# Both heads' last 64 keys in one slot, and early queries centred with tokens on partitions, in a linear-attention and gated-feed-forward kernel

## The chip, the cores and the metric

The kernel runs on one core of one Trainium2 chip. The metric is the device time of one execution in microseconds; three runs of the kernel before gave 1332.12, 1333.95 and 1334.01 (median 1333.95). Lower is better. PE is the matrix engine, PEld its weight loads, DVE the vector engine, ACT the scalar engine, POOL the general engine and SP the engine whose queue issues most DMA transfers.

## The reference

Attention with positive random features, then a gated feed-forward layer, all in float32:

```python
def phi(x):                                   # q, k, v: 8 batches, 8 heads, 576 tokens, 64 wide
    proj = einsum('bhsd,df->bhsf', x, w_phi)  # 128 features
    proj = proj - max(abs(proj), axis=-1, keepdims=True)
    return concatenate([exp(proj), exp(-proj)], axis=-1)
kv = einsum('bhsf,bhsd->bhfd', phi(k), v);  z = sum(phi(k), axis=2)
num = einsum('bhsf,bhfd->bhsd', phi(q), kv)
den = einsum('bhsf,bhf->bhs', phi(q), z) + 1e-06
x = (num / den) as 4608 tokens x 512
out = (silu(x @ w_gate) * (x @ w_val)) @ w_out   # 512 -> 1536 -> 512
```

The largest absolute value is taken over the 128 features of one token, so it is a reduction along the features.

## The kernel before, in words

**Pairs.** Two heads of one batch make a pair; there are 32 (`attention(i, rank)`, L329). Inputs lie with the 2 x 64 head dimensions on partitions, so one pair's keys are a tile `kin` of 128 x 576, its queries `qin` likewise. `wbd` (128 x 256) is the projection as a block diagonal: head 0's features in its first 128 columns, head 1's in the others.

**Keys.** The 576 tokens stand in five slots of 128 that begin at 0, 128, 256, 384 and 448 (`SLOTS`, L30). The last slot overlaps the one before by 64 tokens, whose rows in the value tile `vf` are zero. In three groups (two slots, two, one: `K_GROUPS`) a slot's 128 tokens are the stationary operand and `wbd` streams past (L270 `kin`), DVE takes the largest value (L383) and subtracts it (L388), ACT makes both exponentials (L395), and PE multiplies into the bank `kv` (L407): per slot, head and sign one product of 128 features by 128 columns, 64 of values and 64 of ones. The ones give `z` repeated 64 times, so that the numerators' product also makes the denominators. ACT copies the bank to `kvs` (L417).

**Queries.** `wbd`'s half for a head is stationary and 288 tokens stream, so features lie on partitions (L270 `qin`). ACT copies the four results to `qx` (L449). The largest value over partitions is found by DVE: two 32 x 32 block transposes (L455), a reduction (L459), six small copies and maxima over the partition groups (L462 to L467), a transpose that spreads the result (L471) and the subtraction (L473). ACT makes two exponentials of 128 x 1152 into `qe` and `qx` (L475, L476). Then four numerator products on PE (`kvs`), copies to `num` and `den` on ACT (L514, L516), and on DVE a transpose, a reciprocal, a transpose back and a product (L523 to L527). ACT and DVE split the result into a high and a low part `xh`, `xl` (L539, L541).

**Early and late pairs.** The first eight pairs (`EARLY_PAIRS`) multiply in plain float32. Each such product stands in the trace as two matmul records and two weight loads. The other 24 split operands into high and low parts and multiply three times in the type `fp32r`, one record each; they share only the `kv` product's plain float32 with the early ones. An early pair may use five PSUM banks for work, a late one two.

**The feed-forward layer.** Chunks of 384 tokens go through twelve slices of 128 hidden units. The first layer (`gv`) is 24 matmuls of 384 columns a slice, the second (`o`) nine of 512 columns. Three chunks come from the early pairs. Their first layer runs while the weights, which arrive as float64, are converted: 36 pieces, each with two steps on ACT (L292, L307) and seven on DVE (L293 to L308).

**The order.** `Plan` lays out every engine's instructions ahead of time by simulating them with assumed costs (`dve`, `act`, `pe`, `pe32`). Of the ready steps the one of the lowest rank goes first: a pair's number is its rank, the weights' slices have 3.0, 5.0, 6.5 and up (`W_RANKS`), feed-forward products come after all pairs that are ready. Where PE has nothing, the planner puts in a dummy product (`nothing`, L706 and L708) that keeps PE awake. Each engine then runs its own list in order, so a step that waits holds all behind it.

Of the kernel before, what the change touches and what calls it, by code (L numbers as in the profile page):

```python
# [8 lines left out]
F32 = mybir.dt.float32  # L9
# [20 lines left out]
SLOTS = [0, 128, 256, 384, 448]  # L30
K_GROUPS = [(0, 2), (2, 4), (4, 5)]

# [148 lines left out]
def favor_attention_moe(ctx: ExitStack, tc: tile.TileContext, qT, kT, v, w_phi, wg, wv, wo, out):  # L181
# [23 lines left out]
    kin, qin = [sb("kin", [P, S])] * 2, [sb("qin", [P, S])] * 2  # L205

    vf = [sb("vf", [P, 5, 2, P])] * 2
# [4 lines left out]
    kvl = sb("kvl", [P, 4 * P], F32R)  # L212
    km = sb("km", [P, 4], F32, 4)
# [21 lines left out]
    k_parts = lambda: later("ks", "qx1", [P, 2, S])  # L235
    q_parts = lambda: later("qs", "qe1", [P, 2, S])
    kv_high = lambda: later("kvh", "kvs1", [P, 4 * P])

# [9 lines left out]
    wbd, wst = sb("wbd", [P, 2 * NF]), osb[1][:, :NF]  # L248
# [4 lines left out]
    for hi, lo, w in ((wbd_hi, wbd_lo, wbd), (wst_hi, wst_lo, wst)):  # L253
        nc.scalar.copy(hi, w)
        nc.vector.tensor_tensor(out=lo, in0=w, in1=hi, op=ALU.subtract)
    for h in range(2):
        nc.gpsimd.memset(vf[0][:, :, h, (1 - h) * D:(2 - h) * D], 1.0)
    nc.gpsimd.memset(vf[0][0:D, 4], 0.0)
# [70 lines left out]
    def attention(i, rank):  # L329
# [11 lines left out]
        k_in = add("SP", P * S * 4, lambda: nc.sync.dma_start(kin[j], kT[b, pr]), [last.get(("kin", i - 1))], rank)  # L341
# [11 lines left out]
        if early:  # L353
            k_ready = [k_in]
        else:
            k_hi = add("ACT", act(S), lambda: nc.scalar.copy(k_parts()[:, 0], kin[j]),
                       [k_in, last.get(("khi", i - 1)), *(use("qx") if i == EARLY_PAIRS else ())], rank)
            k_lo = add("DVE", dve(S), lambda: vec.tensor_tensor(
                out=k_parts()[:, 1], in0=kin[j], in1=k_parts()[:, 0], op=ALU.subtract), [k_hi], rank)
            k_ready = [k_hi, k_lo]  # L360
            last["kin", i] = k_lo
        kv_steps = []
        for g, (t0, t1) in enumerate(K_GROUPS):
            w = t1 - t0
            key = ("k", i, g)
            buf = (3 * i + g) % 2
            view = lambda key=key, w=w: work[plan.bank[key]][:, :w * 256].rearrange("p (t f) -> p t f", f=NF)

            def project(t0=t0, t1=t1, key=key):
                o = work[plan.bank[key]]  # L370
                for t in range(t0, t1):
                    c = slice(SLOTS[t], SLOTS[t] + P)
                    acc = o[:, (t - t0) * 256:(t - t0 + 1) * 256]
                    if early:
                        matmuls([(acc, kin[j][:, c], wbd, True, True)])
                    else:
                        khi, klo = (k_parts()[:, n, c] for n in range(2))
                        matmuls([(acc, khi, wbd_hi, True, False), (acc, khi, wbd_lo, False, False),
                                 (acc, klo, wbd_hi, False, True)])

            kproj = add("PE", w * (pe32(256) if early else 3 * pe(256)), project, k_ready, rank, take=key)
            m = km[(3 * i + g) % len(km)]
            kmax = add("DVE", dve(256 * w), lambda w=w, m=m, view=view: vec.tensor_reduce(  # L383
                out=m[:, :2 * w], in_=view(), axis=AX.X, op=ALU.max, apply_absolute_value=True),
                       [kproj, last.get(("km", 3 * i + g - 4))], rank)

            def centre(w=w, m=m, view=view, buf=buf):
                vec.tensor_tensor(  # L388
                    out=kp[buf][:, :w, :, 1].rearrange("p t h f -> p (t h) f"), in0=view(), op=ALU.subtract,
                    in1=m[:, :2 * w].rearrange("p (n o) -> p n o", o=1).broadcast_to([P, 2 * w, NF]))  # L390

            def exponential(s, w=w, buf=buf):
                x = kp[buf][:, :w, :, 1].rearrange("p t h f -> p (t h) f")
                o = kp[buf][:, :w, :, s].rearrange("p t h f -> p (t h) f")
                nc.scalar.activation(o, x, AF.Exp, scale=-1.0 if s else 1.0)  # L395

            ksub = add("DVE", dve(256 * w), centre, [kmax, last.get(("kp", 3 * i + g - 2))], rank, give=key)
            e0 = add("ACT", act(256 * w), lambda f=exponential: f(0), [ksub], rank)
            e1 = add("ACT", act(256 * w), lambda f=exponential: f(1), [e0], rank)
            last["km", 3 * i + g] = ksub  # L400

            def values(t0=t0, t1=t1, buf=buf, g=g):
                for t in range(t0, t1):
                    for h in range(2):
                        for s in range(2):
                            o = ps_kv[:, (2 * h + s) * P:(2 * h + s + 1) * P]
                            nc.tensor.matmul(o, kp[buf][:, t - t0, h, s], vf[j][:, t, h],  # L407
                                             start=t == 0 and h + s == 0, stop=t == 4 and h + s == 2)

            kv = add("PE", 4 * w * pe32(P), values, [e1, *v_in, last.get(("kv", i - 1)), *kv_steps[-1:]], rank)  # L410
# [3 lines left out]
        if early:  # L414
            last["kin", i] = kproj
        last["vf", i] = kv_steps[-1]
        kvc = [add("ACT", act(4 * P), lambda: nc.scalar.copy(kv_high() if split else kvs[j], ps_kv),  # L417
                   [kv_steps[-1], *use("kvs")], rank)]
        if split:
            kvc.append(add("DVE", dve(4 * P), lambda: vec.tensor_tensor(out=kvl, in0=ps_kv, in1=kv_high(), op=ALU.subtract),  # L420
                           kvc, rank))
# [3 lines left out]
        copies, q_lo = [], []  # L425
        for h in range(2):
            ra, rb = rows(h)
            if early:
                lo = q_in
            else:  # L430
# [4 lines left out]
            q_lo.append(lo)  # L435
            for part in range(2):
                key = ("q", i, h, part)
                c = slice(part * SH, (part + 1) * SH)

                def project(h=h, c=c, key=key):  # L440
                    acc = work[plan.bank[key]][:, :SH]
                    if early:
                        matmuls([(acc, wbd[:, h * NF:(h + 1) * NF], qin[j][:, c], True, True)])
                    else:
# [3 lines left out]
                pj = add("PE", pe32(SH) if early else 2 * pe(SH), project, [lo], rank, take=key)  # L448
                copies.append(add("ACT", act(SH), lambda h=h, c=c, key=key: nc.scalar.copy(  # L449
                    qx[j][:, h, c], work[plan.bank[key]][:, :SH]), [pj, *use("qx")], rank, give=key))  # L450
            last["qs", h, i] = pj
        last["qin", i] = pj if early else q_lo[-1]
        flat = lambda t: t.rearrange("p h s -> p (h s)")
        blocks = lambda t: flat(t).rearrange("p (a j) -> p a j", j=32)
        turns = [add("DVE", dve(S), lambda h=h: vec.transpose(qe[j][:, h], qx[j][:, h]),  # L455
                     [*copies[2 * h:2 * h + 2], *use("qe")], rank) for h in range(2)]

        def largest():
            vec.tensor_reduce(out=qm, in_=blocks(qe[j]), axis=AX.X, op=ALU.max, apply_absolute_value=True)  # L459

        def over_groups():
            vec.tensor_copy(qu[0:64], qm[64:128])  # L462
            vec.tensor_tensor(out=qm[0:64], in0=qm[0:64], in1=qu[0:64], op=ALU.max)
            vec.tensor_copy(qu[0:32], qm[32:64])
            vec.tensor_tensor(out=qu[0:32], in0=qm[0:32], in1=qu[0:32], op=ALU.max)
            vec.tensor_copy(qu[32:64], qu[0:32])
            vec.tensor_copy(qu[64:128], qu[0:64])  # L467

        mx = add("DVE", dve(2 * S), largest, turns, rank)
        mg = add("DVE", 6 * 170, over_groups, [mx], rank)  # L470
        back = add("DVE", dve(2 * S), lambda: vec.transpose(  # L471
            blocks(qe[j]), qu.rearrange("p (a o) -> p a o", o=1).broadcast_to([P, 2 * NBL, 32])), [mg], rank)
        qc = add("DVE", dve(2 * S), lambda: vec.tensor_tensor(out=flat(qx[j]), in0=flat(qx[j]), in1=flat(qe[j]),  # L473
                                                              op=ALU.subtract), [back], rank)
        f0 = add("ACT", act(2 * S), lambda: nc.scalar.activation(flat(qe[j]), flat(qx[j]), AF.Exp), [qc], rank)  # L475
# [284 lines left out]
```

## Time and profile before

| what | value |
|---|---|
| median of three runs | 1333.95 us |
| the profiled execution's own time | 1333.89 us |
| its span, first to last instruction | 1331.8 us |
| PE busy | 1289.6 us (97%) |
| DVE busy | 900.7 us (68%) |
| ACT busy | 656.6 us (49%) |
| mean granted PE clock | 0.989 |

Busy times of PE overlap: a matmul's record runs from its start to the end of its way through the array, and the next one starts before that. What one matmul costs in a stream is the distance from its start to the next start, and that is read from the timeline, where consecutive equal instructions are one row with a count. A row's second column is the time from the first start to the last end.

### The profile page before, as it was taken

How to read it: one execution, taken by the hardware profiler on the slowest of the kernel's cores; microseconds unless marked ns; L12 is line 12 of the kernel's file. 1: busy time of each engine (PE TensorE's matmuls, PEld its weight loads, DVE VectorE, ACT ScalarE, POOL GpSimd, SP SyncE). 2: the span in 40 equal slices, each digit the busy share in tenths (PEclk: the TensorE clock that was granted, in tenths of full speed). 3: DMA queues.
4: the chain of work that ended last, by engine and by line, in shares of the span. 5: the costliest groups of instructions: out<-in, count | busy, mean ns of one | idle time of the engine just before them, and what ended most of it. 6: DMA issues, size and time to landing. Idle time of an engine off the chain costs nothing.

```text
span 1331.8 us, 19557 instructions
## 1 busy us (share of the span) xinstructions
PE 1289.6 (97%) x7517; PEld 1204.0 (90%) x7517; DVE 900.7 (68%) x1569; ACT 656.6 (49%) x1255; POOL 1.2 (0%) x7
## 2 busy tenths in 40 slices
PE   7997699999999999999999999999999999999998
PEld 6885599999888899999999999999999999999997
DVE  6999689999777788872487777752277787322222
ACT  5776543333767656661356666541276575221211
POOL 0000000000000000000000000000000000000000
PEclk9998799999999999999999999999999999999999
DMA  4324145554455433344334343344443333344433
GB/s 116 88 85 138 34 139 173 186 174 156 151 164 162 128 109 115 106 140 127 121 122 120 110 148 98 112 138 128 135 128 105 115 119 92 116 147 133 147 120 102
DMA packets 105565, 168.14 MB, mean 126 GB/s; under 512 B 46336, under 2 KB 52736, under 8 KB 105472
## 3 DMA queue, kind: packets, MB, share of 16 engines
q1 hardware_dynamic: 105152, 166.76, 40.8%
q8 instruction: 59, 0.97, 0.3%
q14 instruction: 34, 0.28, 0.1%
q10 hardware_dynamic: 320, 0.13, 0.0%
HBM read 143.26 MB, written 23.59 MB: 125 GB/s over the span
## 4 chain that ended last, share of the span: by engine, by line
PE 89%; DVE 6%; DMA 2%; ACT 1%; issue 1%; ACTq 0%; DVEq 0%
PE gv L270 44%; PE o L270 24%; PE work L270 11%; PE kv L407 10%; DMA w_lo<-wlo_dram 1%; DMA out_dram<-osb 1%; DVE kp L388 1%; DMA kin<-in_kT_dram 1%; DVE qx L473 0%; DVE qe L455 0%; DVE km L383 0%; DVE qm L459 0%; DVE qe L471 0%; PE gv L706 0%; DVE den L525 0%
## 5 line engine op out<-in xcount | busy, mean ns | idle before, releaser
L270 PE MATMUL gv<-xh,w_hi 128*128 128x384 f32 x1152 | 388.6, 337 | 3.1 <-ACT xh L539 1.8
L270 PE MATMUL gv<-xl,w_hi 128*128 128x384 f32 x1152 | 386.9, 336 | 1.2 <-DVE xl L541 1.2
L270 PE MATMUL gv<-xh,w_lo 128*128 128x384 f32 x1152 | 387.3, 336 | 0.0
L270 PEld LDWEIGHTS gv<-xh,w_hi 128*128 128x128 f32 x1152 | 216.8, 188 | 9.8 <-ACT xh L539 3.0
L270 PEld LDWEIGHTS gv<-xl,w_hi 128*128 128x128 f32 x1152 | 216.7, 188 | 6.6 <-DVE xl L541 2.0
L270 PEld LDWEIGHTS gv<-xh,w_lo 128*128 128x128 f32 x1152 | 216.5, 188 | 0.0
L606 ACT ACTIVATE th<-gv 128x384 f32<-128x384 f32 x144 | 70.8, 491 | 266.3 <-PE gv L270 263.1
L608 DVE SCALAR_TENSOR_TENSOR th<-th,gv 128x384 f32<-128x384 f32 x144 | 78.9, 548 | 154.1 <-ACT th L606 153.5
L270 PE MATMUL o<-w_lo,hh 128*128 128x512 f32 x432 | 172.1, 398 | 1.6 <-DMA w_lo<-wlo_dram 1.3
L270 PE MATMUL o<-w_hi,hh 128*128 128x512 f32 x432 | 171.4, 397 | 2.0 <-ACT osb L655 2.0
L270 PE MATMUL o<-w_hi,hl 128*128 128x512 f32 x432 | 171.3, 397 | 0.0
L407 PE MATMUL kv<-vf,kp 128*128 128x128 f32 x1280 | 159.8, 278 | 2.5 <-ACT kp L395 2.5
L407 PEld LDWEIGHTS kv<-vf,kp 128*128 128x128 f32 x1280 | 156.2, 195 | 5.5 <-ACT kp L395 3.2
L631 ACT CAST hh<-th 128x384 fp32r<-128x384 f32 x144 | 73.6, 511 | 164.4 <-DVE th L611 148.7
L611 DVE TENSOR_TENSOR th<-th,gv 128x384 f32<-128x384 f32 x144 | 79.4, 552 | 67.2 <-PE gv L270 64.7
L395 ACT ACTIVATE kp<-kp 128x512 f32<-128x512 f32 (+1 forms) x192 | 105.8, 557 | 28.8 <-DVE kp L388 26.1
L523 DVE STREAM_TRANSPOSE qe<-den 128x576 f32<-128x576 f32 x32 | 24.8, 775 | 132.5 <-ACT den L516 132.5
L632 DVE TENSOR_TENSOR hl<-th,hh 128x384 fp32r<-128x384 f32 x144 | 79.2, 550 | 32.7 <-ACT hh L631 32.1
L270 PEld LDWEIGHTS o<-w_hi,hl 128*128 128x128 f32 x432 | 81.5, 189 | 19.0
L270 PEld LDWEIGHTS o<-w_lo,hh 128*128 128x128 f32 x432 | 81.6, 189 | 16.5 <-DMA w_lo<-wlo_dram 4.1
L270 PEld LDWEIGHTS o<-w_hi,hh 128*128 128x128 f32 x432 | 81.5, 189 | 15.5 <-ACT osb L655 2.8
L514 ACT COPY num<-work 64x288 f32<-64x288 f32 x106 | 41.7, 393 | 56.1 <-PE work L270 54.8
(94 smaller groups left out, 1793.8 us busy)
## 6 DMA issues: line engine op xcount, KB each, us to landing
w_lo<-wlo_dram SPq DMA_DIRECT2D x108, 512.0 KB, 3.5
w_lo<-wlo_dram SPq DMA_DIRECT2D x132, 256.0 KB, 3.0
kin<-in_kT_dram SPq DMA_DIRECT2D x32, 288.0 KB, 3.1
qin<-in_qT_dram SPq DMA_DIRECT2D x32, 288.0 KB, 2.8
wlo_dram<-w_lo SPq DMA_DIRECT2D x36, 256.0 KB, 2.1
out_dram<-osb SPq DMA_DIRECT2D x36, 256.0 KB, 3.0
vf<-in_v_dram SPq DMA_DIRECT2D x64, 128.0 KB, 3.0
shared<-in_wg_dram SPq DMA_DIRECT2D x12, 512.0 KB, 3.5
```

The costliest lines, as they stand in the source:

```text
L270: nc.tensor.matmul(o, l, r, start=a, stop=z)
L388: vec.tensor_tensor(out=kp[buf][:, :w, :, 1].rearrange("p t h f -> p (t h) f"), in0=view(), op=ALU.subtract, in1=m[:, :2 * w].rearrange("p ...
L395: nc.scalar.activation(o, x, AF.Exp, scale=-1.0 if s else 1.0)
L407: nc.tensor.matmul(o, kp[buf][:, t - t0, h, s], vf[j][:, t, h], start=t == 0 and h + s == 0, stop=t == 4 and h + s == 2)
L514: copied.append(add("ACT", act(SH), lambda key=key, ra=ra, c=c: nc.scalar.copy(num[ra, c], work[plan.bank[key]][ra, :SH]), [nu, free], rank))
L523: t0 = add("DVE", dve(S), lambda: vec.transpose(turned, den), [*copied, *done], rank)
L606: s1 = add("ACT", act(CH), lambda: nc.scalar.activation(t_, ps_gv[0][:, :CH], AF.Tanh, scale=0.5), [ends[0], th_free[j]], FIRST)
L608: s2 = add("DVE", dve(CH), lambda: nc.vector.scalar_tensor_tensor(out=t_, in0=t_, scalar=1.0, in1=ps_gv[0][:, :CH], op0=ALU.add, op1=ALU.m ...
L611: s3 = add("DVE", dve(CH), lambda: nc.vector.tensor_tensor(out=t_, in0=t_, in1=ps_gv[1][:, :CH], op=ALU.mult), [s2, ends[1]], FIRST)
L631: s4 = add("ACT", act(CH), lambda: nc.scalar.copy(hh[b], th[j]), [made, hid_free[b]], FIRST)
L632: s5 = add("DVE", dve(CH), lambda: nc.vector.tensor_tensor(out=hl[b], in0=th[j], in1=hh[b], op=ALU.subtract), [s4], FIRST)
```

## The change

The last key slot now holds no token twice. Its 128 rows are head 0's last 64 tokens (rows 0 to 63) and head 1's (rows 64 to 127). In `kin`, now 128 x 640, columns 512 to 575 have head 0's dimensions and zero elsewhere, 576 to 639 head 1's. The stacked projection `wst` (both heads' weights in the same 128 columns) then gives 128 features a token, so the tail's projection, reduction, subtraction and exponentials are half as wide. Values carry two columns of ones in place of 64 (`D2` is 66), and the tail needs one product a sign, of 132 columns. Two ACT copies make `kvs` from the bank: the values, and the sums repeated 64 times. For late pairs the low part (`kvl`) takes two DVE steps likewise. `kin` comes in three transfers.

An early pair's queries go the keys' way: tokens stationary, `wbd` streaming 256 columns (five slots, the last overlapping), reduction and subtraction along the features into `qy`, then PE turns each 128 x 128 block with an identity matrix into PSUM, and ACT's exponentials read it there. DVE's transposes, the small maxima and the copies of the projection are gone from these pairs. Late pairs' queries are as before. The identity is made by POOL at the start, ahead of two of the five memsets of the padding; `wst` has a tile of its own.

```diff
+Q_GROUPS = [(0, 2), (2, 4), (4, 5)]
+SK = 5 * P
+D2 = D + 2
...
-    kin, qin = [sb("kin", [P, S])] * 2, [sb("qin", [P, S])] * 2
-    vf = [sb("vf", [P, 5, 2, P])] * 2
+    kin, qin = [sb("kin", [P, SK])] * 2, [sb("qin", [P, S])] * 2
+    vf = [sb("vf", [P, 5, 2, D2])] * 2
...
+    qy = sb("qy", [P, 4, NF], F32, 2)
+    ident = sb("ident", [P, P])
...
+    make_identity(nc, ident)
...
-        k_in = add("SP", P * S * 4, lambda: nc.sync.dma_start(kin[j], kT[b, pr]), ...)
+        k_in = [add("SP", P * 4 * P * 4, lambda: nc.sync.dma_start(kin[j][:, :4 * P], kT[b, pr, :, :4 * P]), ...)]
+        k_in += [add("SP", P * P, lambda r=slice(h * D, (h + 1) * D), c=4 * P + h * D: nc.sync.dma_start(
+            kin[j][r, c:c + D], kT[b, pr, r, 4 * P:]), ...) for h in range(2)]
...
             def project(t0=t0, t1=t1, key=key, tail=tail):
+                    c = slice(t * P, (t + 1) * P)
+                    acc = o[:, :NF] if tail else o[:, (t - t0) * 256:(t - t0 + 1) * 256]
                     if early:
-                        matmuls([(acc, kin[j][:, c], wbd, True, True)])
+                        matmuls([(acc, kin[j][:, c], wst if tail else wbd, True, True)])
...
             def values(t0=t0, t1=t1, room=room, tail=tail):
+                if tail:
+                    for k in range(2):
+                        nc.tensor.matmul(ps_kv[:, 2 * k * D2:2 * (k + 1) * D2], room[:, 0, k],
+                                         vf[j][:, 4].rearrange("p h d -> p (h d)"), start=False, stop=k == 1)
+                    return
                 for t in range(t0, t1):
                     for h in range(2):
-                            o = ps_kv[:, (2 * h + s) * P:(2 * h + s + 1) * P]
-                            nc.tensor.matmul(o, kp[buf][:, t - t0, h, s], vf[j][:, t, h], ...)
+                            o = ps_kv[:, (2 * k + h) * D2:(2 * k + h + 1) * D2]
+                            nc.tensor.matmul(o, room[:, 2 * (t - t0) + h, k], vf[j][:, t, h], ...)
...
-        kvc = [add("ACT", act(4 * P), lambda: nc.scalar.copy(kv_high() if split else kvs[j], ps_kv), ...)]
+        for ones in range(2):
+            kvc.append(add("ACT", act(4 * D), lambda ones=ones: nc.scalar.copy(
+                cut(kv_high() if split else kvs[j], ones), sums(ones)), ...))
...
+        if early:
+            for g, (t0, t1) in enumerate(Q_GROUPS):
+                    for t in range(t0, t1):
+                        matmuls([(o[:, (t - t0) * 256:(t - t0 + 1) * 256], qin[j][:, SLOTS[t]:SLOTS[t] + P], wbd, True, True)])
+                mx = add("DVE", dve(256 * w), ... vec.tensor_reduce(out=m[:, 4:4 + 2 * w], in_=view(), ...)
+                qc = add("DVE", dve(256 * w), centre, ...)      # qy = projection - largest
+                def turn(w=w, y=y, key2=key2):
+                    for h in range(2):
+                        for t in range(w):
+                            nc.tensor.transpose(o[:, (h * w + t) * P:(h * w + t + 1) * P], y[:, 2 * t + h], ident)
+                f0 = add("ACT", act(2 * size), lambda f=exponential: f(0), [tn, ...], rank)
+                f1 = add("ACT", act(2 * size), lambda f=exponential: f(1), [f0], rank, give=key2)
+        else:
...
```

The planner lays out all lists anew. PE's list where the third pair's projections begin (`kv` is the key-value bank, `o_` and `work_` are PSUM banks for work, `nil` is the dummy), before:

```order
L407 MATMUL kv<-vf,kp_106 128x128 x4
L270 MATMUL o_138<-wbd,kin 128x256 x2
L270 MATMUL o_140<-wbd,kin 128x256 x2
L270 MATMUL o_139<-wbd,kin 128x256
L270 MATMUL work_144<-qin,wbd 128x288
L270 MATMUL work_145<-qin,wbd 128x288
L706 MATMUL gv_142<-wbd_hi,nil 128x256 x2
L270 MATMUL work_144<-qin,wbd 128x288
L270 MATMUL work_145<-qin,wbd 128x288
L706 MATMUL gv_142<-wbd_hi,nil 128x256 x8
```

and in the changed kernel, with the turns through `ident`:

```order
L424 MATMUL kv<-vf,kp_106 128x66 x8
L424 MATMUL kv<-vf,kp_107 128x66 x8
L485 MATMUL o_141<-ident,qy_120 128x128 x4
L279 MATMUL o_142<-wbd,qin 128x256 x2
L279 MATMUL o_140<-wbd,qin 128x256
L279 MATMUL work_146<-wbd,kin 128x256 x2
L279 MATMUL work_147<-wbd,kin 128x256 x2
L417 MATMUL kv<-vf,kp_106 128x132 x2
L279 MATMUL o_141<-wst,kin 128x128
L279 MATMUL gv_143<-xh_97,w_hi_69 128x384
```

Key and query projections now stand between the `kv` products, the turns are spread among them, and the dummies at this place are gone. Over the whole stage of the early pairs the list had 72 dummies and has 20. In both kernels 42 `gv` matmuls stand ahead of the last early pair's numerators.

DVE's list for one early pair's queries, before (the first row is the second block transpose, and L308 and its like would be weight conversion):

```order
L455 STREAM_TRANSPOSE qe_112<-qx_110 128x576
L459 TENSOR_REDUCE qm<-qe_112 128x36
L462 COPY qu<-qm 64x36
L463 TENSOR_TENSOR qm<-qm,qu 64x36
L464 COPY qu<-qm 32x36
L465 TENSOR_TENSOR qu<-qm,qu 32x36
L466 COPY qu<-qu 32x36
L467 COPY qu<-qu 64x36
L471 STREAM_TRANSPOSE qe_112<-qu 128x1152
```

and now (L400 and L405 are the next pair's keys, L469 and L474 the queries):

```order
L469 TENSOR_REDUCE km_116<-o_140 128x4
L474 TENSOR_TENSOR qy_120<-o_140,km_116 128x512
L469 TENSOR_REDUCE km_117<-o_142 128x2
L474 TENSOR_TENSOR qy_121<-o_142,km_117 128x256
L400 TENSOR_REDUCE km_118<-o_141 128x4
L405 TENSOR_TENSOR kp_106<-o_141,km_118 128x4x128
L400 TENSOR_REDUCE km_119<-work_146 128x4
L405 TENSOR_TENSOR kp_107<-work_146,km_119 128x4x128
L400 TENSOR_REDUCE km_116<-work_147 128x1
```

The chain over the partition groups is gone, and the queries' reductions and subtractions stand between the keys'. Up to the last early pair's subtraction both lists hold the same weight conversion: ten pieces are begun.

More of the change, by code (lines that the diff above doesn't have):

```diff
@@ L397, in attention @@
-            ksub = add("DVE", dve(256 * w), centre, [kmax, last.get(("kp", 3 * i + g - 2))], rank, give=key)
-            e0 = add("ACT", act(256 * w), lambda f=exponential: f(0), [ksub], rank)
-            e1 = add("ACT", act(256 * w), lambda f=exponential: f(1), [e0], rank)
-            last["km", 3 * i + g] = ksub
-            def values(t0=t0, t1=t1, buf=buf, g=g):
+                        w_hi, w_lo = (wst_hi, wst_lo) if tail else (wbd_hi, wbd_lo)
+                        matmuls([(acc, khi, w_hi, True, False), (acc, khi, w_lo, False, False), (acc, klo, w_hi, False, True)])
@@ new lines, in attention, with centre @@
+            width = NF if tail else 256
+            kproj = add("PE", w * (pe32(width) if early else 3 * pe(width)), project, k_ready, rank, take=key)
+            m = km[(3 * i + g) % len(km)][:, :n]
+            kmax = add("DVE", dve(n * NF), lambda m=m, view=view: vec.tensor_reduce(
+                out=m, in_=view(), axis=AX.X, op=ALU.max, apply_absolute_value=True),
+                       [kproj, last.get(("km", 3 * i + g - 4))], rank)
+            def centre(n=n, m=m, view=view, room=room):
+                vec.tensor_tensor(out=room[:, :, 1], in0=view(), op=ALU.subtract,
+                                  in1=m.rearrange("p (n o) -> p n o", o=1).broadcast_to([P, n, NF]))
@@ L416, in attention, with cut, sums @@
         last["vf", i] = kv_steps[-1]
[L417 to L418 removed]
+        def cut(t, ones):
+            x = t.rearrange("p (k c d) -> p k c d", k=2, d=D)
+            return x[:, :, 1:3] if ones else x[:, :, 0:4:3]
+        def sums(ones):
+            x = ps_kv[:, :4 * D2].rearrange("p (k h d) -> p k h d", k=2, h=2)
+            return x[:, :, :, D:D + 1].broadcast_to([P, 2, 2, D]) if ones else x[:, :, :, :D]
@@ L434, in attention @@
                     out=q_parts()[rb, h], in0=qin[j][ra], in1=q_parts()[ra, h], op=ALU.subtract), [hi], rank)
[L435 to L444, printed above, removed]
+                q_lo.append(lo)
@@ L445, in project @@
+                for part in range(2):
+                    key = ("q", i, h, part)
+                    c = slice(part * SH, (part + 1) * SH)
+                    def project(h=h, c=c, key=key):
+                        acc = work[plan.bank[key]][:, :SH]
                         x = q_parts()[:, h, c]
                         matmuls([(acc, wst_hi, x, True, False), (acc, wst_lo, x, False, True)])
-                pj = add("PE", pe32(SH) if early else 2 * pe(SH), project, [lo], rank, take=key)
-                copies.append(add("ACT", act(SH), lambda h=h, c=c, key=key: nc.scalar.copy(
-                    qx[j][:, h, c], work[plan.bank[key]][:, :SH]), [pj, *use("qx")], rank, give=key))
@@ L451, in attention @@
[L451 to L475, printed above, removed]
-        f1 = add("ACT", act(2 * S), lambda: nc.scalar.activation(flat(qx[j]), flat(qx[j]), AF.Exp, scale=-1.0), [f0], rank)
+                    pj = add("PE", 2 * pe(SH), project, [lo], rank, take=key)
@@ new lines, in attention @@
+                    copies.append(add("ACT", act(SH), lambda h=h, c=c, key=key: nc.scalar.copy(
+                        qx[j][:, h, c], work[plan.bank[key]][:, :SH]), [pj, *use("qx")], rank, give=key))
+                last["qs", h, i] = pj
+            last["qin", i] = q_lo[-1]
+            blocks = lambda t: flat(t).rearrange("p (a j) -> p a j", j=32)
+            turns = [add("DVE", dve(S), lambda h=h: vec.transpose(qe[j][:, h], qx[j][:, h]),
+                         [*copies[2 * h:2 * h + 2], *use("qe")], rank) for h in range(2)]
```

131 lines of the change are left out of this document (86 added, 45 removed).

## The prediction

> **What bounds the kernel now.** I read the page first: the busy line, then the slices.
>
> ```profile
> span 1331.8 us, 19557 instructions
> PE 1289.6 (97%) x7517; PEld 1204.0 (90%) x7517; DVE 900.7 (68%) x1569; ACT 656.6 (49%) x1255; POOL 1.2 (0%) x7
> PE   7997699999999999999999999999999999999998
> DVE  6999689999777788872487777752277787322222
> PEclk9998799999999999999999999999999999999999
> ```
>
> A slice is 33.3 us. PE is full from the sixth on; only the first five, where the early pairs run, have holes, a lower clock, and a DVE as full as PE. So there are two stages with different limits. The windows put numbers on them (start and end, length, busy us of PE, PEld, DVE, ACT and POOL, then clock, DMA share, GB/s):
>
> ```profile
> 20.00:100.00 80.00, 76.65 (x463) 66.84 (x462) 76.84 (x140) 60.09 (x121) 0.00 (x0) 1.00 0.31 87
> 100.00:161.00 61.00, 40.87 (x173) 30.16 (x171) 49.40 (x92) 36.39 (x72) 0.00 (x0) 0.85 0.29 88
> 161.00:180.00 19.00, 17.26 (x109) 16.94 (x110) 14.23 (x23) 8.90 (x19) 0.00 (x0) 0.84 0.26 73
> 180.00:340.00 160.00, 160.00 (x896) 155.42 (x895) 150.05 (x286) 62.25 (x108) 0.00 (x0) 1.00 0.51 171
> 340.00:450.00 110.00, 105.39 (x609) 90.84 (x608) 85.53 (x142) 74.95 (x142) 0.00 (x0) 0.98 0.52 154
> 450.00:1320.00 870.00, 869.84 (x5169) 826.55 (x5170) 513.66 (x870) 403.14 (x775) 0.00 (x0) 1.00 0.40 123
> ```
>
> From 180 PE sets the time nearly alone: there a change is worth what it takes off PE's stream. Before 161 DVE is busy 96% (20 to 100), then 81%. PE's 76.65 hides dummies and overlapping records, so I counted PE by start-to-start times:
>
> ```profile
> 43.49 0.65 PE L270 MATMUL o<-qe,kvs 128*128 128x288 f32 x2
> 47.38 1.05 PE L407 MATMUL kv<-vf,kp 128*128 128x128 f32 x8
> 48.27 2.11 PE L270 MATMUL o<-wbd,kin 128*128 128x256 f32 x9
> 107.81 0.65 PE L270 MATMUL work<-qx,kvs 128*128 128x288 f32 x2
> 118.89 3.67 PE L407 MATMUL kv<-vf,kp 128*128 128x128 f32 x16
> 122.35 0.79 PE L270 MATMUL o<-qin,wbd 128*128 128x288 f32 x2
> 157.12 0.65 PE L270 MATMUL o<-qx,kvs 128*128 128x288 f32 x2
> 303.36 12.51 PE gv L270 x72
> 700.79 0.28 PE L270 MATMUL work<-wbd_hi,ks 128*128 128x256 f32 x1
> 701.14 0.34 PE L270 MATMUL gv<-xh,w_hi 128*128 128x384 f32 x1
> ```
>
> A pair's 16 numerator records take 47.38 - 43.49 = 3.89 us, 0.243 each; so 256 columns in float32 take 0.243 x 256/288 = 0.216. A `kv` record takes 0.89/8 = 0.111, a `gv` matmul 12.51/72 = 0.174, a late key projection's 0.35/3 = 0.117 (256 columns in fp32r). At 118.89 a `kv` record takes 0.216: the clock is halved there.
>
> The early stage ends with the last pair's numerators, at 157.12 + 0.49 = 157.6. PE's own work until then, for one pair: keys 10 x 0.216 = 2.16, `kv` 40 x 0.111 = 4.44, queries 8 x 0.243 = 1.94, numerators 3.89, together 12.43; eight pairs 99.5, and the 42 `gv` matmuls of the list 7.3: 106.8 us. So 50.8 us of the stage are not work: 7.1 ahead of the first matmul, 72 dummies x 0.117 = 8.4, and 35.3 of waits and slow clock, most of it between 107.81 (sixth pair's last numerators) and the end. The waits name the partner (us in all, times, longest; the last one is DVE idle behind the last pair, whose chain has nothing beside it):
>
> ```profile
> PE gv L706 <- ACT wbd_hi L254: 7.1, 1, 7.1
> PE o L270 <- ACT qe L475: 6.9, 2, 5.4
> DVE qe L523 <- ACT den L516: 9.5, 1, 9.5
> ```
>
> **The change part by part.** First DVE and ACT in an early pair (busy us, mean ns):
>
> ```profile
> L455 DVE STREAM_TRANSPOSE qe<-qx 128x576 f32<-128x576 f32 x64 | 48.4, 766 | 0.2 <-ACT qx L449 0.2
> L459 DVE TENSOR_REDUCE qm<-qe 128x36 f32<-128x1152 f32 x32 | 43.3, 1352 | 1.0
> L463 DVE TENSOR_TENSOR qm<-qm,qu 64x36 f32<-64x36 f32 x32 | 6.0, 187 | 1.1
> L464 DVE COPY qu<-qm 32x36 f32<-32x36 f32 x32 | 5.5, 172 | 1.1
> L471 DVE STREAM_TRANSPOSE qe<-qu 128x1152 f32<-128x1152 f32 x32 | 44.0, 1375 | 0.6
> L473 DVE TENSOR_TENSOR qx<-qx,qe 128x1152 f32<-128x1152 f32 x32 | 43.2, 1350 | 0.3
> L383 DVE TENSOR_REDUCE km<-work 128x4 f32<-128x512 f32 x54 | 36.9, 682 | 0.0
> L388 DVE TENSOR_TENSOR kp<-work,km 128x512 f32<-128x512 f32 x54 | 37.3, 690 | 2.0
> L388 DVE TENSOR_TENSOR kp<-work,km 128x256 f32<-128x256 f32 x24 | 10.1, 423 | 0.9 <-PE kv L407 0.3
> L395 ACT ACTIVATE kp<-kp 128x512 f32<-128x512 f32 x128 | 79.3, 628 | 8.6 <-DVE kp L388 6.8
> L395 ACT ACTIVATE kp<-kp 128x256 f32<-128x256 f32 x64 | 26.5, 414 | 20.2 <-DVE kp L388 19.4
> L449 ACT COPY qx<-work 128x288 f32<-128x288 f32 x116 | 43.5, 401 | 9.7 <-PE work L270 8.6 <-DVE ql L489 0.4
> L475 ACT ACTIVATE qe<-qx 128x1152 f32<-128x1152 f32 x32 | 37.3, 1166 | 37.2 <-DVE qx L473 37.0
> L417 ACT COPY kvs<-kv 128x512 f32<-128x512 f32 x8 | 4.7, 584 | 6.2 <-PE kv L407 6.1
> ```
>
> DVE loses 2 x 0.766 + 1.352 + 6 small steps at about 0.18 + 1.375 + 1.350 = 6.69 us a pair and gains the keys' pattern, 2 x (0.682 + 0.690) + 2 x 0.42 = 3.58. The halved tail saves two steps of 0.133 (the slope between 512 and 256 columns): 0.27. Net -3.38, times eight -27 us. ACT loses four copies of 0.401 and two exponentials of 1.166 (3.94), gains four of 0.628 and two of about 0.31 (3.13), saves 0.2 in the tail and pays 0.24 for the second `kvs` copy: -0.8 a pair. Reading PSUM is no dearer: the copy from PSUM in L449 lies below the line through the two L395 rows.
>
> PE gains work. Per early pair: keys 8 x 0.216 + 2 x 0.111 = 1.95, `kv` 18 products = 36 x 0.111 = 4.00, queries 10 x 0.216 = 2.16, ten turns at 0.111 = 1.11, numerators 3.89: 13.11, or 0.68 more; eight pairs and the `gv` work come to 112.2.
>
> Two prices stand on nothing that runs now. The 66-column `kv` record: streaming alone would take 0.111 x 66/128 = 0.057, but its weight load stays 128 x 128, and a load after idle shows what that takes:
>
> ```profile
> 24.53 0.30 PEld L270 LDWEIGHTS work<-wbd,kin 128*128 128x128 f32 x2 [1.08 <-issue]
> 24.56 0.67 PE L270 MATMUL work<-wbd,kin 128*128 128x256 f32 x2 [0.91 <-DMA kin<-in_kT_dram]
> ```
>
> Two loads of 0.19 span 0.30, so the second begins 0.11 after the first, while the first matmul still streams. 0.11 is also what a 128-column record takes now, a little over the 0.108 that the numerators' rate gives 128 columns: the load already sets it. I take 0.111, with 0.057 as the low end. The turn's load is the same; I take one record of 0.111, with 0.054 and two records (0.222) as ends: -4.6 to +8.9 us over the 80. The Trainium skill's page TensorE: Matmul & The Clock Gate, Part 4, speaks against the turns: about 275 ns each in a kernel. By that estimate the eighty would cost 22 us and the forecast would be 13 us later; no turn runs on PE here yet.
>
> **Early stage.** The loads are now PE 112, DVE (126.2 from 20 to 161) 99, ACT (96.5) 90. PE becomes the fullest. It cannot end before 7.1 + 112.2 = 119.3. DVE as the bound was 96% busy at best and 81% at worst; PE with three nearly even engines lies between, I take 88%: 112.2/0.88 + 7.1 = 134, with 97% (123) and 81% (146) as ends. That is 23.6 us earlier, with the same `gv` work and the same weight conversion behind it. What comes next is not late: from 180 to 340 conversion fills DVE to 150 of 160 us while PE has no hole, and both keep that work unchanged. The two added `kin` transfers, and POOL's identity, lie beside this: the first turn stands behind 16 `kv` products.
>
> **Late pairs.** `kv` loses two products, 4 x 0.111 = 0.444; the tail's three fp32r matmuls of 128 columns cannot beat the load, 3 x 0.006 = 0.02 (if they stream at half, 0.18). 24 x 0.46 = 11.1 us, all on PE's path. DVE and ACT gain and lose a few tenths a pair behind 514 and 403 busy of 870 us: nothing, or about as much per pair if PE had to wait for them. The new `kin` pieces have a whole pair's time.
>
> **Sum.** 1331.8 - 23.6 - 11.1 = 1297.1 for the span. The profiled execution took 1333.89, 2.1 more, and the median is 1333.95. Forecast: **1299 us**.
>
> **Rivals.** *The `kv` record follows its 66 columns* (0.057). For it: nothing shown excludes that a load gets shorter in a denser stream. Against: the 0.11 between two loads. Late pairs would save 24 x 32 x 0.054 = 41.5 us more; in the early stage DVE would hold the end at about 128: 1299 - 41.5 - 6 = 1251. The skill's same page gives both sides: Back-to-back issue gap (columns over 2.4 plus 2.5 ns) makes two passes of 66 columns 57.5 ns by estimate, its LDWEIGHTS section 107 ns for 128 columns; the trace's 0.11 agrees with the second.
>
> *PE waits for its turns.* A turn sits in PE's list ahead of key projections and waits for DVE's subtraction, ACT's exponentials wait for the turn. 24 such groups at 0.7 us (one subtraction each) are 17 us: stage end 151, 1316 us. For it: PE already waited for this chain (6.9 us). Against: the list has other work between subtraction and turn.
>
> *Slower: the clock falls.* In the stage after 100 the mean clock was 0.85, and a halved clock doubles a `kv` record. If loads and turns kept the array so little occupied that it was granted half, 112 us of work would take up to 224. From 70 us at half clock the 34.7 us gained are gone; at 90 us the time is 1299 + 45 = 1344. Against: 20 to 100 ran at 1.00 with 128-column `kv` records. The skill's Part 4 says that turns do not count as PE being busy; no run here shows it.
>
> *No gain on balance*: turns of two records and a stage end near 158, with the late 11 us given back to waits.
>
> **How the numbers follow.** Forecast 0.71, short `kv` record 0.10, waits for turns 0.12, no gain 0.03, slower clock 0.04. The forecast's own ends are 1299 - 11 - 4.6 - 3.8 = 1280 (stage at 123, short turns, short tail) and 1299 + 12 + 9 = 1320; the waits' 1316 lies inside, and about 2 in 10 stay out. The kernel can be told from no change from 0.2% on: faster 0.93, within 0.03, slower 0.04.
>
> **What would show it.** Right: `kv` records of 66 columns 0.11 apart; one record a turn; last early numerators near 134 and PE without holes from 160 on; DVE's busy time down by about 27 us. Wrong: `kv` records under 0.09 apart, holes on PE ahead of turns, a clock under 0.9 before 130, or new holes after 180.

## The result and the profile after

The changed kernel took 1289.66 us (1288.66 to 1290.86, four runs) against 1333.96 (1332.12 to 1334.01) before: a ratio of 0.9672, with a 95% interval of 0.9655 to 0.9688. The forecast was 1299 us, so 35 of the 44 us gained were foreseen and 9 were not. One later execution of the changed kernel, the profiled one of *after_third*, took 1340.93 us at a mean granted clock of 0.897; the 1290.68 us given for that run below is the median without it.

The page of the changed kernel, its busy line and its slices (now 32.2 us each):

```profile
span 1289.1 us, 19542 instructions
PE 1264.5 (98%) x7430; PEld 1189.8 (92%) x7430; DVE 869.3 (67%) x1553; ACT 642.8 (50%) x1287; POOL 1.2 (0%) x11
PE   7999999999999999999999999999999999999998
DVE  6997899997778787772776788742477877322222
PEclk9999899999999999999999999999999999999999
```

The holes of PE's first five slices are gone, and DVE is busy 31 us less. The windows by stage (columns as in the prediction), the first row from the trace of the kernel before, the others from the changed kernel:

```profile
20.00:126.00 106.00, 95.06 (x544) 80.65 (x543) 102.02 (x188) 75.29 (x153) 0.00 (x0) 0.97 0.34 98
```

```profile
20.00:126.00 106.00, 103.45 (x637) 91.88 (x636) 95.99 (x181) 81.40 (x194) 0.00 (x0) 1.00 0.41 114
126.40:136.00 9.60, 5.74 (x23) 5.39 (x23) 7.16 (x12) 5.21 (x12) 0.00 (x0) 0.65 0.12 31
161.00:180.00 19.00, 19.00 (x109) 18.60 (x108) 17.93 (x38) 7.03 (x13) 0.00 (x0) 1.00 0.52 171
180.00:340.00 160.00, 157.23 (x888) 150.24 (x886) 142.98 (x264) 70.98 (x128) 0.00 (x0) 0.99 0.54 170
340.00:450.00 110.00, 107.09 (x622) 95.22 (x621) 82.27 (x144) 70.24 (x142) 0.00 (x0) 0.98 0.50 144
```

The order of the two engines has turned: DVE led with 102 to 95, now PE leads with 103.5 to 96. The timeline gives the prices that the forecast had to bound, and the end of the early stage:

```profile
43.14 0.61 PE L485 MATMUL o<-ident,qy 128*128 128x128 f32 x4
43.59 1.46 PE L279 MATMUL o<-wbd,qin 128*128 128x256 f32 x6
54.44 3.68 PE L424 MATMUL kv<-vf,kp 128*128 128x66 f32 x32
57.96 0.28 PE L485 MATMUL o<-ident,qy 128*128 128x128 f32 x1
125.90 0.65 PE L279 MATMUL o<-qx,kvs 128*128 128x288 f32 x2
128.21 0.38 PE L279 MATMUL work<-wbd_hi,ks 128*128 128x256 f32 x1 [1.66 <-ACT ks L368]
130.91 0.79 PE L279 MATMUL work<-wbd_hi,ks 128*128 128x256 f32 x2 [2.20 <-DVE ks L370]
```

Start to start, four turns take 43.59 - 43.14 = 0.45 us, 0.11 each; 32 `kv` records of 66 columns take 57.96 - 54.44 = 3.52, 0.110 each, the same as 128 columns did. The last early numerators start at 125.90, so the stage ends at 125.90 + 0.49 = 126.4, where the forecast had 134 and the kernel before 157.6. The rest of the span went from 1331.8 - 157.6 = 1174.2 to 1289.1 - 126.4 = 1162.7: 11.5 us less, where 11.1 were forecast. So 31.2 of the 42.7 us that the span lost lie in the early stage. The waits of 1.66 and 2.20 us behind the stage, for the first late pair's key parts, are not new: before, they were 1.6 and 2.2.

Three groups of the changed kernel, and PE's waits between 8 and 126 us, of which these are all:

```profile
L485 PE MATMUL o<-ident,qy 128*128 128x128 f32 x78 | 11.8, 273 | 0.0
L485 PE MATMUL work<-ident,qy 128*128 128x128 f32 x2 | 0.4, 272 | 0.0
L776 PE MATMUL gv<-wbd_hi,nil 128*128 128x256 f32 x20 | 4.2, 356 | 6.8 <-ACT wbd_hi L262 6.8
```

```profile
PE o L279 <- DMA qin<-in_qT_dram: 1.0, 1, 1.0
PE o L279 <- ACT den L586: 0.9, 1, 0.9
PE o L279 <- ACT qx L496: 0.6, 2, 0.4
```

The 78 + 2 turns are 80 records, one each, and no idle time of PE stands ahead of any of them (the last column). From PE's first matmul at 6.8 us it waits 2.5 us for others until the stage ends.

### The profile page after: what moved, and what is told of

It reads as the page before. It is cut to its first block, busy times and chain, and to the rows that moved or that the text cites. A ratio compares the mean times of both kernels' runs of the same rounds, so it can differ in the third digit from the quotient of the medians.

```text
span 1289.1 us, 19542 instructions
## 1 busy us (share of the span) xinstructions
PE 1264.5 (98%) x7430; PEld 1189.8 (92%) x7430; DVE 869.3 (67%) x1553; ACT 642.8 (50%) x1287; POOL 1.2 (0%) x11
## 4 chain that ended last, share of the span: by engine, by line
PE 95%; DMA 2%; DVE 1%; ACT 1%; issue 0%; ACTq 0%; SPq 0%; DVEq 0%
PE gv L279 47%; PE o L279 25%; PE work L279 13%; PE kv L424 9%; PE kv L417 1%; DMA w_lo<-wlo_dram 1%; PE o L485 1%; DMA out_dram<-osb 0%; PE gv L776 0%; DMA qin<-in_qT_dram 0%; DMA wbd<-in_w_phi_dram 0%; DVE qm L529 0%; ACT osb L725 0%; DVE hl L702 0%; DVE qe L525 0%
## 5 line engine op out<-in xcount | busy, mean ns | idle before, releaser
L424 PEld LDWEIGHTS kv<-vf,kp 128*128 128x128 f32 x1024 | 120.9, 192 | 2.5 <-ACT kp L409 1.0
L424 PE MATMUL kv<-vf,kp 128*128 128x66 f32 x1024 | 120.3, 272 | 0.8 <-ACT kp L409 0.6
L279 PE MATMUL work<-qh,kvh 128*128 128x288 f32 x192 | 60.7, 316 | 0.0
## 6 DMA issues: line engine op xcount, KB each, us to landing
vf<-in_v_dram SPq DMA_DIRECT2D x64, 128.0 KB, 2.9
```

Source lines behind the costliest of these rows:

```text
L279: nc.tensor.matmul(o, l, r, start=a, stop=z)
L424: nc.tensor.matmul(o, room[:, 2 * (t - t0) + h, k], vf[j][:, t, h], start=t + h + k == 0, stop=False)
```

## The experiments

**The two parts apart.** *keys_alone* has the new key slot and the narrow values, with the early queries as before:

```
-        if early:
-            for g, (t0, t1) in enumerate(Q_GROUPS):
-                ...                      # tokens on partitions, turns
-        else:
+        copies, q_lo = [], []            # all pairs: projection, copies, DVE transposes
```

> The changed kernel with the early queries as before: only the last key slot is new. My theory (DVE holds the early stage before, PE holds everything after it): late pairs give 24 x 0.46 = 11 us, the early stage only DVE's 0.27 us a pair, 2 us; time 1318 to 1324, last early numerators at 153 to 158. Rival (the fewer PE products are what shortened the early stage): end near 140 and a time under 1310.

*queries_alone* is the kernel before with the early queries of the change (`kvl` shares the memory of a `qy` buffer there):

```
+Q_GROUPS = [(0, 2), (2, 4), (4, 5)]
+    qy = sb("qy", [P, 4, NF], F32, 2)
+    make_identity(nc, ident)
+        if early:
+            for g, (t0, t1) in enumerate(Q_GROUPS):
+                ...                      # project, reduce, centre, turn, exponentials
```

> The kernel before with only the early queries changed (tokens on partitions, turned by PE). My theory: the early stage shortens nearly as in the changed kernel, though PE has 12.43 + 1.33 = 13.76 us a pair, 117.4 in all with gv; at the changed kernel's 94% that is an end at 132, and nothing is gained later: 1304 to 1313. Rival (the gain in the early stage needs both parts): end after 145, time over 1318.

Beside a kernel before of 1333.57 us, *keys_alone* took 1320.31 (ratio 0.99, interval 0.9885 to 0.9914) and *queries_alone* 1305.56 (0.979, 0.9775 to 0.9804). Early numerators and windows of *keys_alone*:

```profile
157.95 0.65 PE L278 MATMUL o<-qx,kvs 128*128 128x288 f32 x2
20.00:126.00 106.00, 95.49 (x528) 79.68 (x527) 101.08 (x188) 74.50 (x159) 0.00 (x0) 0.95 0.36 101
```

and of *queries_alone*:

```profile
129.17 0.65 PE L275 MATMUL o<-qx,kvs 128*128 128x288 f32 x2
20.00:126.00 106.00, 105.09 (x652) 94.55 (x651) 98.83 (x184) 79.97 (x181) 0.00 (x0) 1.00 0.42 118
```

The parts lie in different places. The key slot leaves the stage where it was (158.4) and shortens what follows; the queries shorten the stage to 129.7 and leave what follows at 1304.5 - 129.7 = 1174.8, as before. *keys_alone* takes 8 x (0.21 + 0.44) = 5.2 us from PE in the stage, and the stage ends no earlier: PE's work did not hold it. The 2 us less on DVE were expected to bring the end to 153 to 158, and that did not show either; PE's first query projection starts 1.2 us later there (12.77 against 11.53), the clock from 20 to 126 was 0.95 where 0.97 stood, and these were not separated from DVE's part. Its rest of 1316.7 - 158.4 = 1158.3 is 15.9 us less, 4.8 more than the late products account for; in the windows after the stage its granted clock is 0.92 where 0.85 stood before (158 to 180) and 1.00 where 0.98 stood (340 to 450), which by estimate is about 3.8 us (0.07 of 22 and 0.02 of 110), and why the clock differs there was not tested. The two gains add to 41.3 us, against 44.3 for both together: once the queries have freed DVE, what the keys take off PE shortens the stage as well (129.7 to 126.4).

**What a `kv` record costs.** *load_probe* adds 48 matmuls ahead of the second group of turns in the first four pairs; the turns overwrite their results:

```
+                    if i < 4 and g == 1:
+                        for cols, m, lhs, rhs in ((P, 66, y..), (P, 16, y..), (D, 66, y..), (D, 16, y..),
+                                                  (P, 66, wbd_hi, wst_hi), (D, 66, wbd_hi, wst_hi)):
+                            for _ in range(8):
+                                nc.tensor.matmul(o[:cols, :m], lhs[:, :cols], rhs[:, :m], ...)
```

> The changed kernel with 48 more matmuls ahead of the second group of turns in each of the first four pairs, whose results the turns overwrite: eight each of float32 with 128 stationary columns and 66, then 16 streaming; with 64 stationary columns and 66, then 16 streaming; of fp32r with 128 and with 64 stationary columns and 66 streaming. If the weight load sets the pace (my theory): 0.11 us a record with 128 stationary columns whatever streams, and clearly less, 0.055 to 0.09, with 64. Rival, a fixed cost per record: 0.11 everywhere. Rival, the stream sets it: 66 columns 0.056, 16 columns less.

Windows of the probe's own line in the third pair, PE and PEld only. Each row holds 16 records in float32, of 128 stationary columns with 66 streaming, 128 with 16, 64 with 66, and 64 with 16 (a record or two of the neighbour falls into each count):

```profile
69.53:71.27 1.74, 1.74 (x17) 1.74 (x17) 1.00 0.78 199
71.27:73.10 1.83, 1.83 (x18) 1.80 (x17) 1.00 0.69 182
73.10:74.09 0.99, 0.99 (x18) 0.99 (x18) 1.00 0.11 27
74.09:75.07 0.98, 0.98 (x19) 0.95 (x17) 1.00 0.00 0
```

A record takes about 0.11 us with 128 stationary columns and 0.06 with 64, whether 66 or 16 columns stream, and PEld is full in all four. So at 16 and at 66 streaming columns the weight load sets the pace, and its size alone counts; the fp32r records in the same place took the same. In the other three pairs the granted clock was halved during part of the probe, and there the same records took 0.213 and 0.107: the load follows the clock. The Trainium skill, page TensorE: Matmul & The Clock Gate, section LDWEIGHTS (loading the stationary operand), gives columns over 1.2 in ns for a load: 107 and 53 ns. The rows above, at full clock, give (73.10 - 69.53)/32 = 0.112 us and (75.07 - 73.10)/32 = 0.062, near both.

*wide_values* pads the values from 66 to 104 columns:

```
-D2 = D + 2
+D2 = 104
```

> The changed kernel with 104 columns for values and ones in place of 66 (40 columns of ones): the main kv products stream 104 columns, the tail's 208. If the load sets the pace, the main products do not change and the tail's records go from 0.112 to 0.176: 32 x 4 x 0.064 = 8 us slower than the changed kernel (1296 to 1299). If the narrower columns gave time by themselves: 1024 records would grow too, 20 us or more slower.

It took 1296.98 us (0.9715, 0.9701 to 0.9728) beside 1292.11 for the changed kernel on the same chip. Its timeline:

```profile
40.75 3.71 PE L424 MATMUL kv<-vf,kp 128*128 128x104 f32 x32
44.30 0.60 PE L485 MATMUL o<-ident,qy 128*128 128x128 f32 x4
47.76 0.87 PE L417 MATMUL kv<-vf,kp 128*128 128x208 f32 x4
48.47 0.38 PE L279 MATMUL o<-wst,kin 128*128 128x128 f32 x2
```

The 32 main records still take 3.55/32 = 0.111; only the tail's four grow, from 0.11 to 0.71/4 = 0.178. Over 32 pairs that is 4 x 0.067 x 32 = 8.6 us of PE, of which 4.9 show in the time; the clock from 126.4 to 136 was 0.89 there and 0.66 in the changed kernel beside it, which hides a part. The 62 columns fewer gained nothing by themselves. What counts is that the tail needs two products less, and that its 132 columns stay close to the load.

**Which engine holds the early stage.** *turns_twice* makes each turn two times, 80 x 0.109 = 8.7 us more on PE:

```
-                            nc.tensor.transpose(o[:, (h * w + t) * P:...], y[:, 2 * t + h], ident)
+                            for _ in range(2):
+                                nc.tensor.transpose(o[:, (h * w + t) * P:...], y[:, 2 * t + h], ident)
```

> The changed kernel with each of the 80 turns made twice in a row; lists in the same order, same result. PE has 80 x 0.109 = 8.7 us more in the early stage, DVE and ACT nothing. If PE bounds that stage: 7 to 9 us slower than the changed kernel (about 1297 to 1299). If DVE bounds it: under 3 us slower (about 1290 to 1293).

*dve_twice* makes each reduction of the early queries two times, 14.2 us more on DVE:

```
+                def largest(w=w, m=m, view=view):
+                    for _ in range(2):
+                        vec.tensor_reduce(out=m[:, 4:4 + 2 * w], in_=view(), ...)
```

> The changed kernel with each reduction of the early queries made twice; lists in the same order, same result. DVE has 8 x (2 x 0.68 + 0.42) = 14.2 us more in the early stage, PE and ACT nothing. If PE bounds that stage and DVE has the slack that its share leaves (96 busy of 106 us from 20 to 126): 0 to 5 us slower than the changed kernel (1290 to 1295). If DVE bounds it: 11 to 15 us slower (1301 to 1305).

They took 1298.3 us (0.9734, 0.9719 to 0.9748) and 1300.85 (0.9749, 0.9733 to 0.9765), where the changed kernel's ratio is 0.9672. Last numerators and windows of the stage, *turns_twice*:

```profile
134.75 0.65 PE L279 MATMUL o<-qx,kvs 128*128 128x288 f32 x2
20.00:135.00 115.00, 113.83 (x728) 102.22 (x725) 97.94 (x184) 83.92 (x200) 0.00 (x0) 1.00 0.38 107
```

*dve_twice*:

```profile
138.40 0.65 PE L279 MATMUL o<-qx,kvs 128*128 128x288 f32 x2
20.00:138.00 118.00, 109.25 (x642) 91.51 (x641) 110.32 (x207) 83.38 (x195) 0.00 (x0) 1.00 0.37 104
```

The stage ends 8.8 us later for 8.7 on PE, and 12.5 later for 14.2 on DVE. Part of this is not the added work. PE's first eight key-projection records run partly at half clock, for a stretch that differs from run to run, and they come ahead of everything that these experiments change. The changed kernel, then *no_reduction* (a run described below):

```profile
8.71 2.39 PE L279 MATMUL o<-wbd,kin 128*128 128x256 f32 x8
10.94 0.38 PE L279 MATMUL o<-wst,kin 128*128 128x128 f32 x2
```

```profile
8.50 3.62 PE L281 MATMUL o<-wbd,kin 128*128 128x256 f32 x8
11.91 0.61 PE L281 MATMUL o<-wst,kin 128*128 128x128 f32 x2
```

The eight take 10.94 - 8.71 = 2.23 us in the one and 11.91 - 8.50 = 3.41 in the other, 0.43 each, twice the 0.216 of full clock. So the ends are better compared from the first query projection on, which follows these records (the end is the end of the last numerators' record less 0.65 - 0.49 = 0.16):

| run | first query projection at | stage ends at | between | beside the changed kernel |
|---|---|---|---|---|
| changed kernel | 11.16 | 126.39 | 115.2 | |
| *after_again*, the same kernel | 11.11 | 126.37 | 115.3 | 0.0 |
| *turns_twice*, PE + 8.7 | 12.94 | 135.24 | 122.3 | +7.1 |
| *dve_twice*, DVE + 14.2 | 12.24 | 138.89 | 126.7 | +11.4 |
| *no_reduction*, DVE - 14.2 | 12.34 | 127.97 | 115.6 | +0.4 |
| *half_numerators*, PE - 15.5 | 11.79 | 123.77 | 112.0 | -3.3 |
| *both_less* | 11.23 | 118.42 | 107.2 | -8.0 |
| *query_tail* | 11.95 | 124.89 | 112.9 | -2.3 |

Either addition costs some four fifths of itself, so the theory that PE alone holds the stage with DVE's slack to spare fell. Two theories were left: two engines side by side, both nearly full, or one chain that runs through both in turn. Additions cannot tell these apart; reductions can. From two full engines, less work on one gains little and less on both gains much; on one chain each gains by itself, and the gains add.

*no_reduction* leaves out the early queries' reductions, with a constant subtracted in place of the largest magnitude:

```
+    nc.vector.memset(fixed, 6.0)
-                mx = add("DVE", ..., vec.tensor_reduce(...))
+                mx = add("DVE", ..., lambda w=w, m=m, view=view: None,
-                        in1=m[:, 4:4 + 2 * w]...
+                        in1=fixed[:, :2 * w]...
```

> The changed kernel with the early queries' reductions left out: a fixed 6.0 is subtracted in place of each token's largest value. DVE has 14.2 us less in the early stage, all else and all lists' order alike. After doubled turns (last early numerators 8.9 us later for 8.7 us of PE) and doubled reductions (12.5 later for 14.2 of DVE), two theories are left. Two full engines side by side (each would set about the same end alone): taking work from DVE alone leaves PE's bound, 0 to 4 us earlier. One chain that runs through both engines in turn (what either does is waited for by the other): 8 to 12 us earlier.

*half_numerators* leaves out the second product, that of the negative exponentials, of each early numerator: 64 records of 0.243, 15.5 us of PE:

```
+                    terms = terms[:1] if not split else terms
```

> The changed kernel with the second of the two products (negative exponentials) left out of the early pairs' numerators: PE has 8 x 8 x 0.243 = 15.5 us less in the early stage, all else and all lists' order alike. Two full engines side by side: DVE's bound stays, 0 to 4 us earlier. One chain through both: 10 to 14 us earlier.

*both_less* leaves out both.

> Both of these left out in one kernel. Two full engines side by side: only now the stage shortens, 10 us or more and clearly beyond the sum of the two alone. One chain: about the sum of the two alone, until ACT (96 of the 106 us at most) holds it.

Beside a kernel before of 1335.44 us and the changed kernel at 1290.68 (*after_third*: 0.9659, 0.9642 to 0.9676) they took 1291.55 (0.9666, 0.965 to 0.9682), 1285.9 (0.963, 0.9616 to 0.9645) and 1281.94 (0.9601, 0.9586 to 0.9615). Windows and last numerators of *no_reduction*:

```profile
127.48 0.65 PE L281 MATMUL o<-qx,kvs 128*128 128x288 f32 x2
20.00:126.00 106.00, 103.03 (x636) 91.72 (x635) 85.80 (x162) 81.13 (x193) 0.00 (x0) 1.00 0.41 116
```

of *half_numerators*, with the largest of PE's waits:

```profile
121.52 2.41 PE L279 MATMUL o<-qe,kvs 128*128 128x288 f32 x8
20.00:126.00 106.00, 95.35 (x577) 79.08 (x575) 96.37 (x183) 83.47 (x199) 0.00 (x0) 1.00 0.41 115
PE o L279 <- DVE kp L405: 2.4, 3, 1.3
```

and of *both_less*:

```profile
116.17 2.41 PE L281 MATMUL o<-qe,kvs 128*128 128x288 f32 x8
20.00:118.00 98.00, 91.92 (x573) 80.80 (x572) 84.17 (x161) 79.84 (x192) 0.00 (x0) 0.98 0.44 124
```

With 14.2 us off DVE the stage ends at 128.0, 1.6 later than 126.4, of which 1.2 is the start: nothing gained, PE as full as ever. With 15.5 off PE it ends at 123.8, 2.6 earlier (3.3 by the table), and PE now waits 8.1 us for others, 5.0 of them for DVE, where it waited 2.5. With both off it ends at 118.4, 8.0 earlier, where the two alone give 1.0 together (2.9 by the table). One chain through both would have given the sum of the two, so that theory falls, and two engines side by side stand. Side by side, 10 us or more had been expected of *both_less*, and 8.0 came. A clock of 0.98 over 98 us accounts for at most 2 by estimate; ACT is busy 79.8 of the 98 us, and whether it comes next was not tested. In time *half_numerators* gains 4.8 us, so about 2 of it lie behind the stage; its clock from 340 to 450 was 1.00, where the changed kernel's was 0.98.

**A further step.** *query_tail* gives the early queries' last 64 tokens the keys' arrangement too: both heads' tokens in one slot, projected by `wst` into 128 columns, one turn in place of two, half the reduction and subtraction.

```
+            q_in += [add("SP", P * P, lambda ...: nc.sync.dma_start(qin[j][r, c:c + D], qT[b, pr, r, 4 * P:]), ...)]
+                tail = t1 == 5
+                nb = 1 if tail else 2 * w
+                        matmuls([(acc, qin[j][:, t * P:(t + 1) * P], wst if tail else wbd, True, True)])
+                    if tail:
+                        nc.tensor.transpose(o[:, :P], y[:, 0], ident)
+                        return
```

> The changed kernel, and the early queries' last slot holds both heads' last 64 tokens as the keys' does: a projection of 128 columns, one turn in place of two, reduction and subtraction half as wide, two more small transfers a pair. Per early pair PE saves 2 x 0.105 + 0.11 = 0.32 us and DVE 0.27: 2.2 to 2.6 us faster than the changed kernel if the stage is bound by PE or DVE, about 1287. Rival (the early stage is bound by its chain and the order of its lists): within 1 us or slower.

The changed kernel ran beside it (*after_again*):

> The changed kernel beside the others on the same chip: 1288.5 to 1291.

*query_tail* took 1287.2 us (0.9644, 0.9631 to 0.9658) and *after_again* 1292.11 (0.9676, 0.9663 to 0.9689): 4.9 us less. *after_again* itself came out above its expectation, and the changed kernel's medians on three occasions are 1289.66, 1290.68 and 1292.11, so about half of the 4.9 is within their spread. *query_tail*'s last numerators, and the windows just behind the stage, first *query_tail*:

```profile
124.40 0.65 PE L280 MATMUL o<-qx,kvs 128*128 128x288 f32 x2
124.90:161.00 36.10, 31.41 (x190) 30.33 (x190) 30.23 (x57) 16.18 (x34) 0.00 (x0) 0.95 0.37 115
```

then *after_again*, whose stage ends at 126.4:

```profile
126.00:161.00 35.00, 30.31 (x178) 28.93 (x177) 28.16 (x50) 15.54 (x33) 0.00 (x0) 0.90 0.34 103
```

The end of the stage is only 1.5 us earlier; from the first query projection on it is 2.3, about what PE or DVE saves (2.2 to 2.6 expected). By estimate at most 1.7 of the 4.9 are the better clock in the 35 us behind the stage (0.95 against 0.90) and 1.1 the clock from 340 to 450 (0.98 against 0.97). No run controlled the clock, so the step is worth about 2 us by these traces, and not 4.9.

## Why the prediction was right, and where it was off

**The bound.** Right: before, the early stage was not PE's, and with the change PE became the fullest engine. *queries_alone* shows the first best: PE got 8 x 1.33 = 10.6 us more to do there, and the stage ended 28 us earlier, with DVE's long way to the queries' largest value gone. How much of that was DVE's busy time and how much the waits and the low clock in that chain was not separated. *no_reduction* shows the second.

**The early stage, 134 against 126.4.** This is the term that was mis-sized. The step was: PE's 112.2 us at a share of 88%, midway between DVE's best and worst as a bound. (The sum gives 112.2/0.88 + 7.1 = 134.6, so 134 is rounded down.) Measured, 112.2 of 126.4 - 6.8 = 119.6 us is 94%. The stage is 6.8 of start, 112.2 of work, 20 dummies x 0.117 = 2.3, and 5.1 of everything else. Two things set PE here apart from DVE as the bound before: it waited only 2.5 us for others, and the granted clock stayed at 1.00 from 20 to 126, where 0.85 had stood after 100. The floor of 119.3 held; the share was a choice between two values of another engine in another order, and it came out too low. The planner's new list of PE was already there to be read, with 20 dummies in place of 72 and, in the stretch shown, other work around the turns; it pointed to few waits, though it gives no share by itself.

**The late pairs, 11.1 against 11.5.** Right in its mechanism: the records stay at the load's 0.11, and the gain is the two products a pair. That the size agrees to 0.4 us is partly luck, for it is a net: from 180 to 340 PE lost 2.8 us to holes where it had lost none, and from 340 to 450 it lost 2.9 instead of 4.6; *keys_alone* shortened the same part by 15.9, *queries_alone* by nothing. The new holes after 180 were named as a sign of being wrong. They did appear: a wait of 1.9 us for a transfer of `w_lo` and one of 0.9 for ACT's `osb`. Before, waits of this kind (1.3 and 1.8) stood behind 340, so most of this has moved forward with the work: PE's holes from 180 to 450 are 5.7 us, and were 4.6.

**DVE.** 27 us less were counted; 31.4 came. The count was of the early pairs alone; in the late ones the halved tail saves 24 x 0.27 = 6.4, while `kvl` in two steps and the wider `ks` cost 2.5 and 1.6 more; the other 2 were not traced.

**The turn.** One record of 0.11, the value taken, with 0.054 and 0.222 as the ends. A turn's record lasts 273 ns on the mean, but the next one starts 0.11 us after it began, and with 80 turns among the other products the clock was 1.00 from 20 to 126. The Trainium skill's page TensorE: Matmul & The Clock Gate, Part 4, gives about 275 ns for a bf16 transpose in a kernel; that agrees with the record here and is not what a turn costs in this stream.

**The rivals.** *The `kv` record follows its 66 columns*: fell by 0.110 here and by the probe. *PE waits for its turns*: fell, 0.0 idle ahead of them. *The clock falls*: did not occur in the early stage (1.00 from 20 to 126), though in *load_probe* (below) it fell during streams of loads with few columns. *No gain on balance*: fell.

One thing the prediction did not say: that DVE would be only some 3 us behind PE. It holds DVE's 99 us against PE's 112, which reads like slack. But the two are not counted alike: the 99 begin at 20 us, the 112 at PE's first matmul. From there to the end of the stage the changed kernel has

```profile
6.80:126.40 119.60, 117.02 (x718) 104.31 (x718) 106.03 (x201) 88.64 (x209) 0.00 (x0) 1.00 0.42 118
```

so DVE is busy 106.0 us, beside PE's 112.2 of work and 2.3 of dummies. *half_numerators* shows how little slack that leaves: with 15.5 us off PE the stage shortens by only 3.3.

## What to carry to other kernels

A matmul whose stationary operand has 128 columns costs its load, 0.11 us here, with 16, 66, 104 or 128 columns streaming, so narrowing the streaming side below 128 gained nothing and leaving out whole products gained all. When two engines are nearly full side by side, as here, work added to either costs most of itself and work taken from one gains little: test with reductions, one at a time and then together, since additions cannot tell two full engines from one chain. Compare ends from a point behind the start, where the clock differs from run to run. For the share at which a new bound will run, read its waits out of the new order of its own list, not the share at which the old bound ran.

## What the runs showed of the hardware

The granted clock fell under a PE that was never idle. Windows of *load_probe* over its streams in the first four pairs:

```profile
17.50:25.50 8.00, 8.00 (x83) 7.95 (x82) 1.58 (x4) 1.43 (x4) 0.00 (x0) 0.86 0.40 104
43.00:52.30 9.30, 9.30 (x82) 9.21 (x80) 2.60 (x5) 0.04 (x1) 0.00 (x0) 0.73 0.29 77
69.50:76.40 6.90, 6.90 (x82) 6.84 (x80) 2.76 (x5) 0.14 (x1) 0.00 (x0) 1.00 0.40 103
91.30:101.00 9.70, 9.70 (x83) 9.64 (x81) 2.91 (x6) 0.11 (x1) 0.00 (x0) 0.69 0.29 74
```

PE and PEld are full in all four, and in three of them the clock was halved for part of the stretch (0.86, 0.73, 0.69), so that 6.9 us of work took up to 9.7. In windows of 2 us the clock is 0.50 from 24 to 30, from 48 to 56 and from 96 to 104, so it stayed halved after the streams had ended (25.5, 52.3 and 101.0). The streams were loads with 16 or 66 columns each; that the array itself, mostly empty then, is what the clock follows is only a guess. The changed kernel's `kv` groups of 3.5 us, with 66 columns, did not bring it about. Which column count and which length do was not tested.
